# An added semaphore wait on GpSimd for VectorE's port instructions, in a fused attention, gated FFN and expert kernel

## The chip, the cores and the metric

The kernel runs on one core of a Trainium2 chip. The core has five engines with an instruction queue each: TensorE (PE, matrix products; PEld is its weight load), VectorE (DVE), ScalarE (ACT), GpSimd (POOL) and SyncE (SP, which issues the DMA transfers). Each queue runs in order, and the queues wait for one another by semaphores. The metric is the time of one execution on the device in microseconds, from runs on the chip.

## The reference

Three layers in float32 follow one another: causal attention with 12 heads, a gated feed-forward layer with a convolution over the sequence, and a sparse layer of four attention experts, of which each token takes the best two.

```python
B, H, S, D = 4, 12, 448, 64                      # batch, heads, sequence, head dimension
attn = softmax(mask(q @ k.T / 8)) @ v            # causal
x = attn as (B, S, 768)
h = relu(x @ w_in)                               # 768 -> 1024
conv = sum(conv_w[k] * shift(h, k - 1) for k in range(3))
x = (h * sigmoid(conv)) @ w_out                  # 1024 -> 768
logits = x @ w_gate                              # top 2 of 4 experts
for e in range(4):
    a = softmax(mask((x @ wq[e]) @ (x @ wk[e]).T / 8))
    out += gate[e] * (a @ (x @ wv[e]) @ wo[e])
```

## The kernel before

Every product in full precision is made of three products of rounded parts: a tensor is split into a high part (a rounded copy, helper `high`, L666 and the lines after it, shown as L670, L672 or L674 for ACT, DVE or POOL) and a low part (the remainder, helper `low`, L678). So beside every matmul there are copies and subtractions, and the kernel spreads them over ACT, DVE and POOL.

The work per batch is: six pairs of heads (`attention`), the feed-forward layer (`ffn_in`), the projections for the experts with w_out folded in (`project`), the experts (`experts`) and the output product (`output`). For one pair of heads, `scores` makes the scores on PE (L734), DVE masks them and takes the row maximum (L711, with the scores in PSUM as one input), ACT takes the exponentials and their sums (L715), DVE adds and inverts the sums (L753, L755), and the normalization is spread as eight to ten small multiplications over ACT (L760) and DVE or POOL (L763). `weigh` transposes the result on PE (L781), copies the transposes out of PSUM (ACT L670, DVE L672) and multiplies with the values (L814). L966 is the line of the three-part products.

In the first batch the weights are also unpacked from 64-bit words by three DVE instructions each (L885, L887, L889) and split into `slab` tiles; the parts are written to a scratch in HBM by SP (L907) and read back for later batches. In the feed-forward layer the convolution is done on DVE (L995) or ACT (L990), with the tanh on ACT (L1010) and the gate on DVE (L1003) or POOL (L1000, L1001).

The order of all this isn't that of the source. Every piece of work is noted as an operation (`P.op`) with the engines that could run it, a planned cost for each, what it reads and writes, and a `port`: a string with "V" in it for the DVE operations that the planner keeps apart from POOL's, and always with "G". The planner (`Plan.schedule`) then lays the operations in time, one list for each engine. An operation whose engine is in its `port` starts in the plan only when the last such operation, on either engine, has ended (L479, L518). So in the plan DVE's port operations and POOL's operations never overlap. On the chip nothing enforces that: the instructions are issued in the order of planned start times (L390, L391), and each engine then runs its own queue, waiting only for the data and buffers it needs.

DVE operations with "V" in their port are the copies, scalings and subtractions between SBUF tiles (those whose costs come from `copy_cost`, `scale_cost` and `two_cost`), the unpacking, the convolution and the gate. Operations with a PSUM input, such as L711 and the copies out of PSUM, have only "G".

Of the kernel before, what the change touches and what calls it, by code (L numbers as in the profile page):

```python
# [166 lines left out]
def noise(seed, n):  # L167

    x = (n * 2654435761 + seed * 40503 + 12345) & 0xFFFFFFFF
    for shift, factor in ((15, 0x2C1B3C6D), (12, 0x297A2D39), (15, 1)):  # L170
        x = ((x ^ x >> shift) * factor) & 0xFFFFFFFF
    return x / 2147483648.0 - 1.0
# [43 lines left out]
class Plan:  # L216
# [135 lines left out]
    def run(self):  # L352


        self.links()
        left = [(b, b.left) for t in self.tags.values() for b in t.made]
        kinds = {id(t.kind): (t.kind, dict(t.kind.free)) for t in self.tags.values()}

        def forward(rank):
            for b, n in left:  # L360
                b.left, b.ap = n, None
                for k in b.banks or ():
                    k.end, k.engine = 0.0, None
            for t in self.tags.values():
                t.next = t.live = 0
            for k, tiles in kinds.values():
                k.free = dict(tiles)
            return self.schedule(rank)

        rank = self.longest()  # L370
        length = forward(rank)
        best = (length, rank)
        for _ in range(ROUNDS):
            if length == float("inf"):
                break
            rank = self.backward()
            length = forward(rank)
            best = min(best, (length, rank))
        rank = list(best[1])
        forward(rank)  # L380
        begin = [o.start for o in self.ops]
        for seed, lo, hi, amp in SHIFTS:
            for o in self.ops:
                if seed < 0:
                    rank[o.n] += amp * (lo <= o.n < hi)
                elif lo <= begin[o.n] < hi:
                    rank[o.n] += amp * noise(seed, o.n)
        if SHIFTS and forward(rank) >= best[0]:
            forward(best[1])
        for o in sorted(self.ops, key=lambda o: (o.start, o.n)):  # L390
            o.fn(o.engine)  # L391

    def schedule(self, rank):
        for o in self.ops:
# [135 lines left out]
def on_scalar(n):  # L530
    return 0.05 + n / 1200


def on_vector(n):
    return 0.067 + n / 960
# [10 lines left out]
class Cost(dict):  # L546


    port = "V"
# [28 lines left out]
def attention_moe_moe(ctx: ExitStack, tc: tile.TileContext, qk, vv, w_in, cw, w_out, wqk, wvg, wo, out):  # L578
    nc = tc.nc
    ctx.enter_context(tc.manual_schedule())  # L580
    P = Plan()

    w1d = nc.dram_tensor("w1_scratch", (NF, 128, 2 * DM), F32, kind="Internal").ap()
    wod = nc.dram_tensor("wo_scratch", (2, 128, 2 * DM), F32, kind="Internal").ap()
# [65 lines left out]
    for name, kind, quota in (  # L650
# [9 lines left out]
            ("po", bank, PO), ("pf", sums, 2), ("fill", sums, 1)):  # L660
        P.tag(name, kind, quota)

# [20 lines left out]
    def scores(qk, j, e):  # L683
# [4 lines left out]
        whole = isinstance(qk, list)  # L688
        sbs = [{3: P.buf("sx"), 2: P.buf("sy")} for _ in range(2)]
        for sb in sbs:  # L690
            sb[0], sb[1] = sb[3], sb[2]
        st = P.buf("st")

        def bank(o, c):
            return sbs[o][c][:QN[c], COL[c]:COL[c] + Q0[c] + QN[c]]
# [5 lines left out]
        def kc(o, c):  # L701
            n = Q0[c] + QN[c]
            return slice(S - n, S) if o else slice(0, n)

        def weight(o, c):
# [11 lines left out]

            P.op({"V": on_vector(w)}, mx, r=[(sb[c], c)], w=[(e, (o, c)), (st, ("m", o, c))])
            P.op({"A": on_scalar(w) + 0.23}, ex, r=[(st, ("m", o, c))], w=[(e, (o, c)), (e, ("x", o, c)), (st, ("s", o, c))])

        if whole:
            for o, (qs, kh, r) in enumerate(qk):
                for c in ORDER:
                    w = Q0[c] + QN[c]
                    P.op({"T": 4 * w / 2400}, lambda _, o=o, c=c, w=w, qs=qs, kh=kh: nc.tensor.matmul(
                        bank(o, c), qs()[:, Q0[c]:Q0[c] + QN[c]], kh()[:, kc(o, c)], start=True, stop=True), r=r, w=[(sbs[o][c], c)])
# [490 lines left out]
```

## Time and profile before

| what | value |
|---|---|
| time, median of 3 runs | 534.32 us (533.75 to 536.55) |
| profiled execution, its own time | 535.11 us |
| its span, first to last instruction | 533.3 us |
| PE busy | 515.4 us (97%) |
| DVE busy | 421.6 us (79%), 1300 instructions |
| ACT busy | 357.7 us (67%) |
| POOL busy | 112.0 us (21%), 132 instructions |
| mean granted clock of TensorE | 0.992 |
| chain that ended last | PE 47%, DVE 25%, ACT 8%, issue 2% of the span |

The profiled execution is 0.8 us longer than the median of the runs. A busy time counts a moment once however many instructions overlap. PE's ends are modelled, so a busy PE isn't a PE at its peak; but its idle times are the time that another engine could give back. The chain that ended last runs through PE for long stretches and changes to DVE and ACT between them. A row of the timeline gives the start in us from the start of the span, the duration, the engine, the line, the operation, what it writes and reads with shapes, how many instructions are merged, and in brackets how long the engine was idle before it and which engine's instruction ended that.

### The profile page before, as it was taken

The page shows a single profiled execution, that of the slowest core. Times are in us where ns is not written, and L with a number is a line of the kernel's source. Part 1 is how long each engine was busy: PE and PEld are TensorE (multiplying, and loading weights), DVE is VectorE, ACT ScalarE, POOL GpSimd, SP SyncE. Part 2 cuts the span into 40 slices and gives each one's busy share as a digit, 9 for nine tenths or more (in the row PEclk, how much of TensorE's full clock was granted, in tenths as well). Part 3 has the DMA queues.
Part 4 walks back from the last instruction along what each step waited for, and adds up shares of the span by engine and source line. Part 5 has one row for each costly group of instructions (what it writes and reads, how often), then busy time and mean ns, then how long its engine had stood idle before and what let it go on. Part 6 is the DMA issues. An engine that isn't in the chain of part 4 may idle for free.

```text
span 533.3 us, 10436 instructions
## 1 busy us (share of the span) xinstructions
PE 515.4 (97%) x3554; PEld 436.2 (82%) x3556; DVE 421.6 (79%) x1300; ACT 357.7 (67%) x1058; POOL 112.0 (21%) x132
## 2 busy tenths in 40 slices
PE   8799999899899999899999999999999999999997
PEld 4678888778689898798898777998987778989875
DVE  6999599889798549999259999986389999842581
ACT  2876279789986557686249986755488867732572
POOL 3152017334232021160012511101114000000010
PEclk9999999899989999999999999999999999999999
DMA  9984246845587011374201573763003315610042
GB/s 239 256 222 135 63 149 195 255 120 206 167 246 201 23 36 37 139 250 163 68 2 46 146 219 84 249 215 87 1 1 113 117 49 194 221 59 1 10 154 104
DMA packets 63381, 69.92 MB, mean 131 GB/s; under 512 B 36576, under 2 KB 57312, under 8 KB 63328
## 3 DMA queue, kind: packets, MB, share of 16 engines
q1 hardware_dynamic: 63328, 69.26, 42.7%
q8 instruction: 28, 0.46, 0.4%
q14 instruction: 25, 0.20, 0.1%
HBM read 55.87 MB, written 13.37 MB: 130 GB/s over the span
## 4 chain that ended last, share of the span: by engine, by line
PE 47%; DVE 25%; ACT 8%; issue 2%; ACTq 0%; DVEq 0%
PE pf L966 34%; DVE e L711 7%; DVE e L763 5%; PE bank L814 5%; DVE z L672 4%; PE bank L781 3%; ACT e L715 3%; PE bank L734 3%; ACT e L760 2%; DVE pair L678 1%; DVE pair L672 1%; DVE work L995 1%; PE bank L966 1%; ACT z L670 1%; PE pf L1074 1%
## 5 line engine op out<-in xcount | busy, mean ns | idle before, releaser
L966 PE MATMUL pf<-pair,slab 128*128 128x448 f32 (+2 forms) x984 | 218.5, 368 | 4.3 <-ACT hp L984 2.7
L966 PEld LDWEIGHTS pf<-pair,slab 128*128 128x128 f32 x984 | 171.8, 189 | 22.2 <-ACT hp L984 3.7
L715 ACT ACTIVATE e<-e,stat 128x192 f32<-128x192 f32 (+3 forms) x256 | 127.1, 499 | 23.8 <-DVE stat L711 23.4
L711 DVE CUSTOM_DVE_ANT_0 e<-bank,mask 128x448 f32<-128x448 f32 (+3 forms) x256 | 92.1, 414 | 6.7 <-PE bank L734 6.5
L966 PE MATMUL pf<-pair,wqks 128*128 128x448 f32 x384 | 81.1, 369 | 0.0
L966 PEld LDWEIGHTS pf<-pair,wqks 128*128 128x128 f32 x384 | 71.4, 188 | 7.0 <-ACT pair L670 0.3
L781 PE MATMUL bank<-ident,e 128*128 128x128 f32 x448 | 70.7, 280 | 6.4 <-DVE stat L711 3.5
L678 POOL TENSOR_TENSOR pair<-work,pair 128x448 fp32r<-128x448 f32 (+1 forms) x39 | 48.6, 1260 | 105.6 <-PE bank L734 39.1
L781 PEld LDWEIGHTS bank<-ident,e 128*128 128x128 f32 x448 | 52.7, 142 | 16.9 <-DVE stat L711 3.6
L672 DVE COPY z<-bank 64x128 f32<-64x128 f32 (+2 forms) x121 | 48.7, 429 | 20.9 <-PE bank L781 16.7
L670 ACT ACTIVATE z<-bank 64x128 f32<-64x128 f32 (+2 forms) x135 | 45.8, 367 | 13.4 <-PE bank L814 7.4
L760 ACT ACTIVATE e<-e,stat 64x64 f32<-64x64 f32 (+3 forms) x116 | 49.4, 454 | 7.5 <-DVE stat L755 5.9
L734 PE MATMUL bank<-pair,pair 64*128 64x448 f32 (+3 forms) x576 | 49.6, 291 | 0.1
L814 PE MATMUL bank<-z,block 128*64 128x448 f32 (+3 forms) x384 | 48.7, 395 | 0.0
L715 ACT ACTIVATION_READ_ACCUMULATOR e<-e,stat 128x1 f32 (+1 forms) x256 | 48.5, 189 | 0.0
L995 DVE SCALAR_TENSOR_TENSOR work<-hp,cws,work 128x448 f32<-128x448 f32 x64 | 43.7, 694 | 3.9 <-ACT work L990 3.3
L734 PEld LDWEIGHTS bank<-pair,pair 64*128 64x128 f32 (+1 forms) x576 | 41.9, 172 | 3.3 <-issue 1.6
L814 PEld LDWEIGHTS bank<-z,block 128*64 128x64 f32 x384 | 27.3, 139 | 20.6 <-issue 11.5
L966 PE MATMUL pf<-wvs,pair 128*128 128x260 f32 x288 | 37.3, 286 | 0.0
L678 DVE TENSOR_TENSOR pair<-pf,pair 64x448 fp32r<-64x448 f32 (+1 forms) x24 | 15.0, 623 | 26.7 <-ACT pair L670 26.4
L966 PEld LDWEIGHTS pf<-wvs,pair 128*128 128x128 f32 x288 | 35.5, 188 | 0.3
L670 ACT ACTIVATE pair<-pf 64x448 fp32r<-64x448 f32 (+1 forms) x24 | 12.8, 541 | 32.3 <-PE pf L966 32.0
(99 smaller groups left out, 593.7 us busy)
## 6 DMA issues: line engine op xcount, KB each, us to landing
slab<-w_scratch SPq DMA_DIRECT2D x24, 768.0 KB, 4.6
work<-in_w_out SPq DMA_DIRECT2D x8, 768.0 KB, 4.8
work<-in_w_in SPq DMA_DIRECT2D x8, 768.0 KB, 5.7
w_scratch<-slab SPq DMA_DIRECT2D x8, 768.0 KB, 4.5
work<-in_qk SPq DMA_DIRECT2D x48, 112.0 KB, 3.4
work<-in_qk SPq DMA_DIRECT2D x24, 224.0 KB, 4.3
out<-work SPq DMA_DIRECT2D x24, 224.0 KB, 2.1
slab<-wo_scratch SPq DMA_DIRECT2D x6, 768.0 KB, 4.3
```

The source lines that it names most:

```text
L670: nc.scalar.activation(dst(), src(), AF.Copy)
L672: nc.vector.tensor_copy(dst(), src())
L678: return lambda e: engine(e).tensor_sub(dst(), src(), f32(h()))
L711: nc.vector.tensor_tensor_reduce(out=ec(o, c), in0=bank(o, c), in1=m, scale=-0.125, scalar=3.0e38, op0=OP.add, op1=OP.min, accum_out=st[ro ...
L715: nc.scalar.activation(ec(o, c), ec(o, c), AF.Exp, bias=st[rows, 0, o, c:c + 1], scale=-1.0, accum_out=st[rows, 1, o, c:c + 1])
L734: nc.tensor.matmul(bank(o, c), q(s)[own, Q0[c]:Q0[c] + QN[c]], k(t)[own, kc(o, c)], start=i == 0, stop=i == 2)
L760: nc.scalar.activation(dst(), src(), AF.Copy, scale=st[rows, 3, o, c:c + 1])
L763: engine(en).tensor_scalar(dst(), src(), st[rows, 3, o, c:c + 1], gate, op0=OP.mult, op1=OP.mult)
L781: P.op({"T": TURN}, lambda _: nc.tensor.transpose(dst(), src(), ident[:, :]), r=r, w=keys)
L814: nc.tensor.matmul(ps[own, S - n:S], v(k, o), z[:, 1024 * o + n0:1024 * o + n0 + n], start=k == 0, stop=k == 3)
L966: nc.tensor.matmul(out_ap(), a(), b(), start=first, stop=end), r=r, w=[(ps, 0)])
L995: return lambda _: nc.vector.scalar_tensor_tensor(cv[:, :S], hp[:, i:S + i], cws[:, fc, i:i + 1], cv[:, :S], op0=OP.mult, op1=OP.add)
```

## The change

When the program is written out in the planned order, the last DVE operation with "V" in its port is remembered. Each POOL operation whose planned start is less than 3 us behind the planned start of that DVE operation gets a dependency on the last instruction of it: the first POOL instruction of the operation waits by semaphore for that DVE instruction to be done. Nothing in the plan, in the order on any engine or in the work itself changes. DVE gets no wait for POOL.

```diff
+        body, near = self.nc.cur_bb.bb, None
         for o in sorted(self.ops, key=lambda o: (o.start, o.n)):
+            n = len(body.instructions)
             o.fn(o.engine)
+            new = body.instructions[n:]
+            if o.engine == "V" and "V" in o.port:
+                near = o, new[-1].name
+            elif o.engine == "G" and near and near[0].start > o.start - 3:
+                self.tc.add_manual_dep(new[0], near[1], mybir.DependencyInfo(mybir.DependencyClass.Sync, mybir.DependencyReason.DATA), reason="port")
@@
     P = Plan()
+    P.tc, P.nc = tc, nc
```

## Rows read from the trace of the kernel before

**Rows 1.** The page, part 1: busy us, share of the span, instructions of each engine

```profile
PE 515.4 (97%) x3554; PEld 436.2 (82%) x3556; DVE 421.6 (79%) x1300; ACT 357.7 (67%) x1058; POOL 112.0 (21%) x132
```

**Rows 2.** Windows: length, busy us (instructions) by engine, PEclk, DMA share, GB/s

```profile
100.00:150.00 50.00, 45.67 (x286) 37.55 (x287) 44.05 (x110) 43.46 (x122) 16.70 (x16) 0.93 0.60 187
```

**Rows 3.** Timeline of PE where it paused: start, us, [idle before, what ended it]

```profile
101.95 1.49 PE L781 MATMUL bank<-ident,e 128*128 128x128 f32 x6 [1.57 <-DVE pair L678]
...
131.03 1.29 PE L966 MATMUL pf<-pair,slab 128*128 128x448 f32 x5 [0.94 <-ACT hp L984]
...
144.87 0.47 PE L966 MATMUL pf<-pair,slab 128*128 128x448 f32 x1 [1.80 <-ACT hp L984]
...
217.16 1.14 PE L781 MATMUL bank<-ident,e 128*128 128x128 f32 x8 [1.38 <-DVE stat L711]
...
423.83 0.91 PE L781 MATMUL bank<-ident,e 128*128 128x128 f32 x6 [0.91 <-DVE stat L711]
```

**Rows 4.** Windows of PE alone: length, PE busy, PEclk, DMA share, GB/s

```profile
102.00:104.00 2.00, 2.00 (x9) 0.51 1.01 366
...
146.00:150.00 4.00, 3.99 (x18) 0.57 0.64 225
```

**Rows 5.** Timeline of POOL and DVE at 98 us; DVE's groups by form (busy, mean ns)

```profile
97.74 2.05 POOL L678 TENSOR_TENSOR slab<-work,slab 128x768 fp32r<-128x768 f32 x1 [0.29 <-ACT slab L670]
...
98.00 1.83 DVE L763 TENSOR_SCALAR e<-e,stat 64x64 f32<-64x64 f32 x1
...
L763 DVE TENSOR_SCALAR e<-e,stat 64x64 f32<-64x64 f32 x33 | 9.9, 306 | 1.0 <-ACT e L760 0.4
```

**Rows 6.** Timelines of POOL, DVE and ACT near 120 us; DVE's group of that form

```profile
119.92 1.84 POOL L678 TENSOR_TENSOR slab<-work,slab 128x768 fp32r<-128x768 f32 x1 [4.38 <-ACT slab L670]
122.25 1.86 POOL L678 TENSOR_TENSOR slab<-work,slab 128x768 fp32r<-128x768 f32 x1 [0.49 <-DVE slab L672]
...
120.12 2.05 DVE L672 CAST slab<-work 128x768 fp32r<-128x768 f32 x1
...
122.32 0.46 ACT L760 ACTIVATE e<-e,stat 128x192 f32<-128x192 f32 x1 [0.86 <-DVE stat L755]
...
L672 DVE CAST slab<-work 128x768 fp32r<-128x768 f32 x2 | 2.6, 1302 | 0.0
```

**Rows 7.** Timelines of POOL, DVE and PE near 214 us; two of DVE's groups

```profile
213.14 0.52 POOL L763 TENSOR_SCALAR e<-e,stat,coef 64x64 f32<-64x64 f32 x1
...
213.51 1.48 DVE L763 TENSOR_SCALAR e<-e,stat,coef 64x64 f32<-64x64 f32 x1
...
215.29 0.48 PE L781 MATMUL bank<-ident,e 128*128 128x128 f32 x2
...
L763 DVE TENSOR_SCALAR e<-e,stat,coef 64x64 f32<-64x64 f32 x28 | 9.5, 356 | 0.4
...
L711 DVE CUSTOM_DVE_ANT_0 e<-bank,mask 128x448 f32<-128x448 f32 x64 | 37.7, 615 | 4.6 <-PE bank L734 4.5
```

**Rows 8.** Timelines of POOL, DVE and PE near 420 us; DVE's group of that form

```profile
419.93 0.68 POOL L763 TENSOR_SCALAR e<-e,stat 128x384 f32<-128x384 f32 x1 [7.17 <-DVE stat L755]
...
420.07 0.65 DVE L763 TENSOR_SCALAR e<-e,stat 128x192 f32<-128x192 f32 x1
...
421.25 0.25 DVE L763 TENSOR_SCALAR e<-e,stat 64x64 f32<-64x64 f32 x1
...
421.53 0.38 PE L781 MATMUL bank<-ident,e 128*128 128x128 f32 x2
...
L763 DVE TENSOR_SCALAR e<-e,stat 128x192 f32<-128x192 f32 x16 | 6.0, 381 | 0.2
```

**Rows 9.** Timelines of POOL and DVE at 26 us

```profile
26.24 2.54 POOL L678 TENSOR_TENSOR pair<-work,pair 128x772 fp32r<-128x772 f32 x1 [6.99 <-ACT pair L670]
...
26.13 0.96 DVE L889 SCALAR_TENSOR_TENSOR work<-work 128x768 int32<-128x768 int32 x1
```

**Rows 10.** Timeline of POOL at 112 us

```profile
112.28 0.94 POOL L674 TENSOR_SCALAR pair<-work 128x896 fp32r<-128x896 f32 x1
```

## The prediction

> **What bounds the kernel now.** I read the busy times first. TensorE (PE) is busy for 515.4 of 533.3 us [rows 1], so a change on DVE and GpSimd (POOL) can give back little more than the time in which PE stands still. I then asked PE's timeline for the larger pauses, because each names who ended it [rows 3]: 1.57 us before 101.95 (ended by DVE), 0.94 and 1.80 us before 131.03 and 144.87 (ACT), 1.38 us before 217.16 and 0.91 us before 423.83 (DVE). Two of the five lie where three engines are full at once: between 100 and 150 us PE is busy for 45.67, DVE for 44.05 and ACT for 43.46 of 50 us [rows 2]. In that stretch the granted clock is 0.93, which is 50 x 0.07 = 3.5 us of full speed lost. It falls in two places, right behind the pause of 1.57 us (0.51 from 102 to 104) and right behind that of 1.80 us (0.57 from 146 to 150) [rows 4]: PE ran for a while at 1.2 instead of 2.4 GHz. The second drop costs 4 x 0.43 = 1.7 us, which leaves some 1.7 us for the first.
>
> Last I looked at what held DVE just before its pauses, and each time it was a POOL instruction running beside it. A norm of 64x64 takes 306 ns in the mean of 33; without the longest the mean is (33 x 0.306 - 1.83) / 32 = 0.26 us. That longest one took 1.83 us, from 98.00 to 99.83, while a POOL subtraction ran from 97.74 to 99.79 [rows 5]. A copy into slab took 2.05 us from 120.12, beside a POOL instruction that began 0.20 us earlier and ended at 121.76; the only other one of that form took 2 x 1.302 - 2.05 = 0.55 us [rows 6]. A norm with coef took 1.48 us where the other 27 took 0.31 [rows 7]. It goes the other way when DVE is first: POOL's subtraction at 26.24 began 0.11 us behind a DVE instruction that ended at 27.09, and took 2.54 us [rows 9]; its neighbour at 119.92, about as wide, took 1.84 [rows 6]. Whoever comes second stands still until the first is done.
>
> The Trainium skill (SBUF — State Buffer, Who interferes with whom) says the same: GpSimd and VectorE share a pair of ports as an exclusive lock for a whole instruction, and issue order decides who blocks. The rows agree. By that rule alone the wait changes who blocks, not how much; this is the first rival below.
>
> **What the change does.** It removes and reorders nothing. In the plan's order 121 POOL operations are issued and 70 of them stand less than 3 us of planned time behind a DVE instruction that can take the ports. Eleven of the 70 already wait, directly or through an earlier POOL instruction, for that DVE instruction or a later one. For the other 59 the wait is new. POOL is in order, so everything behind a waiting instruction waits too. The wait itself costs about 0.08 us: the POOL instruction at 122.25 already waits for the slab copy that ended at 122.17 [rows 6]. On POOL, which is busy 112 us of 533 [rows 1], that is covered unless PE waits for the result at once.
>
> **Place 1, 97.74 us.** POOL's subtraction now waits for the last of DVE's norms. DVE gets back 1.83 - 0.26 = 1.57 us, so the norms, the copy and the subtraction that PE waits for at 101.95 come that much sooner. PE paused for 1.57 us [rows 3]; I take 1.5. POOL's subtraction begins about 1.5 us later: the norm of 98.00 then ends near 98.3, two more norms follow, and the wait ends near 99.2. Its result is written out by SP's queue, and behind that write stand the next loads of q and k; POOL copies those at 112.28, and without an idle time before it [rows 10], so I take 1.5 us as covered there. If that cover were gone, POOL would read them up to 1.5 us late.
>
> **The clock behind it.** With the pause gone, nothing that I see in the rows is left to send PE to 1.2 GHz at 102. Bounds are 0 (it falls there all the same) and 1.7 us; I take 1.7, because both drops in this stretch come behind a long pause [rows 4]. The second drop stays in the sum: the pause of 1.80 us in front of it is ACT's.
>
> **Place 2, 119.92 us.** DVE's copy into slab is freed of 2.05 - 0.55 = 1.5 us. What waits for DVE next is ACT, which stood for 0.86 us before 122.32 [rows 6]; beyond that ACT is its own limit up to 144. Bounds 0 and 0.86; I take 0.8, near the upper end, since the row names DVE's reciprocal as what ended the wait and that sits right behind the copy. It comes out of PE's 0.94 us before 131.03. The two POOL subtractions move by some 0.8 and 0.3 us (1.84 each, from 120.7 instead of 119.92). PE's pauses behind them name ACT and not POOL [rows 3], so POOL was in time there; by how much no row here says, and the worst, that the gain of 0.8 is lost again, is the bound of 0.
>
> **Place 3, 213.5 us.** DVE's norm is freed of 1.48 - 0.31 = 1.17 us, directly in front of the scores that PE's pause of 1.38 us waits for through ACT. I take 1.15. POOL's three norms move by about as much. The first of them ends at 213.66 now and PE transposes it in a pair from 215.29 [rows 7], so it stays in time.
>
> **Place 4, 420 us.** A norm that took 0.65 us, (16 x 0.381 - 0.65) / 15 = 0.36 otherwise, is freed of 0.29 us in front of a pause of 0.91 [rows 3, 8]. I take 0.3.
>
> **What it costs.** In the first 40 us POOL splits weights that PE wants at once. At 26.24 POOL would begin at 27.09 + 0.08 and need 1.84 us instead of ending at 28.78, so it ends 0.2 us later, and so does the one behind it. Bounds 0 and 0.4; I take 0.2. Elsewhere POOL works ahead of the plan, and what it is held back by there I take as covered, since no larger pause of PE names POOL [rows 3]; what it costs without that cover is the second rival.
>
> The sum is 1.5 + 1.7 + 0.8 + 1.15 + 0.3 - 0.2 = 5.25, say 5.2 us. The profiled execution took 535.1 us, 0.8 more than the median of the runs shown (534.3). So the same execution would take 529.9, and the median 529.1.
>
> **Rivals.** *The lock is handed on.* POOL now begins just as the near DVE instruction ends, and then blocks the next DVE instruction instead; DVE loses again what it gained, and the time is 533.5 to 534.3. For it: both engines still want the same ports, and nothing makes DVE wait for POOL. Against it: behind the norms come the score reductions, and these keep their time whatever POOL does (64 of the widest average 615 ns [rows 7]). I give it 0.20.
>
> *POOL too late for PE* (the slower side). A head's norms are split over POOL and DVE, and PE transposes POOL's share in order. At 421.25 the last DVE norm begins and lasts 0.25 us. Held until 421.50 + 0.08, POOL's norm of 0.68 us ends at 422.26, but PE transposes it at 421.53 now [rows 8]: 0.7 us lost. This decides wherever DVE's norm does not itself come forward. Were four heads hit like this (my choice), with none of the gains, it would be 534.3 + 2.8 = 537. Against it: at place 3 there are 1.6 us to spare, and there and at place 4 DVE's norms do come forward. I give it 0.12.
>
> *The clock falls all the same.* The pauses go, but TensorE spends another stretch at 1.2 GHz somewhere else, 1.7 us: 530.8. I give it 0.10. *The wait does nothing*, because the DVE instruction had always ended: 534.3. The rows of the four places speak against it; 0.02.
>
> **How the numbers follow.** The forecast has the remaining 0.56. Its own range is 527.0 (the second clock drop goes as well, by a shift of its pause, 1.7 us, the cost in the first 40 us does not arise, 0.2, and place 3's pause of 1.38 goes whole, 0.2) to 531.6 (the first clock drop stays and place 2 gives nothing). A measurement of this kernel can tell about 0.5% from no change, 2.7 us. Faster by more than that, under 531.6: 0.56 + 0.10 = 0.66. Within: 0.20 + 0.02 = 0.22. Slower: 0.12. The range from 527.0 to 535.0 leaves out the slower rival and the tail of the forecast below it, together under 0.2.
>
> **What would show it.** In the profile after, DVE's norm near 98 us should take about 0.3 us and its copy into slab near 120 us about 0.55 us. PE should have no pause over 0.3 us near 100 us, and its clock there should be 1.00. The pause near 216 us should shrink below 0.4 us, and the one before 145 us should stay. The time that POOL waits for DVE should rise, without PE waiting for POOL. I am wrong if score reductions or slab subtractions now show the stretched durations, or if PE's pauses name POOL.

## The result, and the profile after

The kernel after takes 527.05 us (median of 4 runs, 526.54 to 527.90), the kernel before 534.15 (median of 4 runs, 533.75 to 536.55): a ratio of 0.9852, 95% interval 0.9825 to 0.9879. The gain of 7.1 us is in the direction of the forecast and 1.9 us larger than its 5.2; the time lies at the lower edge of the range. As a ratio to before it lies below it (527.0 of 534.32 is 0.9863). The profiled execution took 527.07 us, 8.0 less than that of before.

The helper lines in the kernel after are eight higher than before (L763 is now L771, L711 is L719, L678 is L686, L672 is L680, L781 is L789, L966 is L974). The first part of the page, to be held against [rows 1]:

```profile
PE 511.8 (97%) x3556; PEld 434.1 (83%) x3556; DVE 413.7 (79%) x1300; ACT 357.0 (68%) x1058; POOL 104.4 (20%) x132
```

DVE is busy for 7.9 us less and POOL for 7.6 us less, with the same work. What POOL spent as a stretched instruction it now spends idle, in front of the instruction. The second thing to see is PE: 3.6 us less busy time and, since the span fell by 8.0, 4.4 us less standing still. The two have different causes. The standing still is read from PE's timeline, the rows with a pause at the places of [rows 3] (start, us, in brackets the idle time before and what ended it):

```profile
126.80 3.92 PE L974 MATMUL pf<-pair,slab 128*128 128x448 f32 x18 [0.23 <-ACT hp L992]
...
140.63 0.47 PE L974 MATMUL pf<-pair,slab 128*128 128x448 f32 x1 [1.88 <-ACT hp L992]
...
210.46 1.14 PE L789 MATMUL bank<-ident,e 128*128 128x128 f32 x8 [0.59 <-DVE stat L719]
```

The pause of 1.57 us near 100 us and that of 0.91 near 423 have no row any more, 0.94 has become 0.23, 1.38 has become 0.59, and ACT's pause of 1.80 is still there (1.88). One more is gone that [rows 3] doesn't list; in the timeline of PE before it was:

```profile
304.07 1.09 PE L781 MATMUL bank<-ident,e 128*128 128x128 f32 x8 [0.56 <-DVE stat L711]
```

Together that is 1.57 + 0.71 + 0.79 + 0.56 + 0.91 = 4.5 us. Not all of it is gained. In the list of what PE waited for, which leaves out waits under 0.15 us, no line names POOL. But near 414 us PE's weight load (PEld) for the second pair of transposes, which had no wait in the trace of before, now waits for POOL's norm:

```profile
414.70 0.20 PEld L789 LDWEIGHTS bank<-ident,e 128*128 128x128 f32 x2 [0.40 <-POOL e L771]
```

From the first of these transposes to the six behind the old pause PE needed 2.79 us before (421.04 to 423.83) and needs 2.25 now (413.95 to 416.20). So of the pause of 0.91 us only 0.54 is gained.

The 3.6 us of PE's busy time are nearly all the clock. The window of [rows 2], with its columns, shows the full clock throughout, so also behind the pause of 1.88 us that stayed:

```profile
100.00:150.00 50.00, 47.83 (x330) 40.21 (x331) 43.58 (x113) 46.81 (x130) 18.11 (x17) 1.00 0.66 201
```

Lined up instruction by instruction, the lead of PE over the kernel before grows by 1.6 us behind the pause near 100 us, and by another 1.65 behind the pause near 143 us, which is as long as it was. These are the two stretches at 1.2 GHz of [rows 4]; the profiled execution of before had both of them and that of after neither.

On DVE and POOL, the rows that answer to [rows 5 to 8], with two rows of before behind them (97.48 and 419.77):

```profile
98.94 1.83 POOL L686 TENSOR_TENSOR slab<-work,slab 128x768 fp32r<-128x768 f32 x1 [1.56 <-ACT z L678]
...
97.08 1.72 DVE L771 TENSOR_SCALAR e<-e,stat 128x192 f32<-128x192 f32 x6
...
116.60 0.56 DVE L680 CAST slab<-work 128x768 fp32r<-128x768 f32 x1
...
206.41 1.09 POOL L771 TENSOR_SCALAR e<-e,stat,coef 128x320 f32<-128x320 f32 x2 [18.78 <-DVE e L771]
208.83 1.67 POOL L771 TENSOR_SCALAR e<-e,stat,coef 64x64 f32<-64x64 f32 x3 [1.32 <-DVE e L771]
...
207.05 1.58 DVE L771 TENSOR_SCALAR e<-e,stat,coef 64x64 f32<-64x64 f32 x4 [0.26 <-POOL e L771]
...
412.69 1.18 DVE L771 TENSOR_SCALAR e<-e,stat 128x320 f32<-128x320 f32 x4
...
97.48 3.22 DVE L763 TENSOR_SCALAR e<-e,stat 128x192 f32<-128x192 f32 x6
419.77 1.72 DVE L763 TENSOR_SCALAR e<-e,stat 128x320 f32<-128x320 f32 x4
```

Near 97 us six norms of DVE (merged in one row, which shows the shape of the first) take 1.72 us; the same six took 3.22 in the trace of before. POOL's subtraction starts behind them, at 98.94, and takes 1.83 us. The copy into slab takes 0.56 us where it took 2.05. Four norms near 413 us take 1.18 us where they took 1.72. By form, the small norms of DVE fell from 306 and 356 ns [rows 5, 7] to 247 and 317, and the score reduction did not move (615 ns [rows 7], now 617):

```profile
L771 DVE TENSOR_SCALAR e<-e,stat 64x64 f32<-64x64 f32 x33 | 8.0, 247 | 0.6
L771 DVE TENSOR_SCALAR e<-e,stat,coef 64x64 f32<-64x64 f32 x28 | 8.4, 317 | 0.6 <-POOL e L771 0.3
...
L719 DVE CUSTOM_DVE_ANT_0 e<-bank,mask 128x448 f32<-128x448 f32 x64 | 37.7, 617 | 5.7 <-PE bank L742 5.6
```

### The profile page after: what moved, and what is told of

Its sections match the earlier page's. It is cut to its first block, busy times and chain, and to the rows that moved or that the text cites. A ratio compares the mean times of both kernels' runs of the same rounds, so it can differ in the third digit from the quotient of the medians.

```text
span 525.3 us, 10440 instructions
## 1 busy us (share of the span) xinstructions
PE 511.8 (97%) x3556; PEld 434.1 (83%) x3556; DVE 413.7 (79%) x1300; ACT 357.0 (68%) x1058; POOL 104.4 (20%) x132
## 4 chain that ended last, share of the span: by engine, by line
PE 49%; DVE 22%; ACT 7%; issue 2%; DMA 1%; POOL 1%; POOLq 0%; ACTq 0%; DVEq 0%
PE pf L974 38%; DVE e L719 6%; DVE z L680 4%; PE bank L822 4%; DVE e L771 4%; PE bank L789 3%; PE bank L742 3%; ACT e L768 2%; ACT e L723 2%; DVE pair L686 1%; PE bank L974 1%; ACT z L678 1%; DMA work<-in_qk 1%; DVE pair L680 1%; PE pf L1082 1%
## 5 line engine op out<-in xcount | busy, mean ns | idle before, releaser
L974 PE MATMUL pf<-pair,slab 128*128 128x448 f32 (+2 forms) x984 | 218.2, 368 | 3.5 <-ACT hp L992 2.1
L974 PEld LDWEIGHTS pf<-pair,slab 128*128 128x128 f32 x984 | 171.2, 188 | 21.7 <-ACT hp L992 2.6
L719 DVE CUSTOM_DVE_ANT_0 e<-bank,mask 128x448 f32<-128x448 f32 (+3 forms) x256 | 92.2, 415 | 7.6 <-PE bank L742 7.4
L974 PE MATMUL pf<-pair,wqks 128*128 128x448 f32 x384 | 80.7, 368 | 0.0
L974 PEld LDWEIGHTS pf<-pair,wqks 128*128 128x128 f32 x384 | 71.6, 188 | 6.3
L789 PE MATMUL bank<-ident,e 128*128 128x128 f32 x448 | 69.5, 277 | 2.5 <-DVE stat L719 1.2
L686 POOL TENSOR_TENSOR pair<-work,pair 128x448 fp32r<-128x448 f32 (+1 forms) x39 | 47.2, 1223 | 101.9 <-PE bank L742 39.4
L680 DVE COPY z<-bank 64x128 f32<-64x128 f32 (+2 forms) x121 | 48.6, 428 | 19.6 <-PE bank L789 15.4
L789 PEld LDWEIGHTS bank<-ident,e 128*128 128x128 f32 x448 | 52.2, 140 | 12.5 <-DVE stat L719 1.6
L678 ACT ACTIVATE z<-bank 64x128 f32<-64x128 f32 (+2 forms) x135 | 45.7, 367 | 10.4 <-PE bank L822 6.8
L822 PE MATMUL bank<-z,block 128*64 128x448 f32 (+3 forms) x384 | 47.1, 386 | 0.0
L974 PE MATMUL pf<-wvs,pair 128*128 128x260 f32 x288 | 37.3, 286 | 0.0
L686 DVE TENSOR_TENSOR pair<-pf,pair 64x448 fp32r<-64x448 f32 (+1 forms) x24 | 15.0, 623 | 26.7 <-ACT pair L678 26.4
L974 PEld LDWEIGHTS pf<-wvs,pair 128*128 128x128 f32 x288 | 35.5, 188 | 0.3
L678 ACT ACTIVATE pair<-pf 64x448 fp32r<-64x448 f32 (+1 forms) x24 | 12.8, 540 | 32.4 <-PE pf L974 32.1
```

Source lines behind the costliest of these rows:

```text
L678: nc.scalar.activation(dst(), src(), AF.Copy)
L680: nc.vector.tensor_copy(dst(), src())
L686: return lambda e: engine(e).tensor_sub(dst(), src(), f32(h()))
L719: nc.vector.tensor_tensor_reduce(out=ec(o, c), in0=bank(o, c), in1=m, scale=-0.125, scalar=3.0e38, op0=OP.add, op1=OP.min, accum_out=st[ro ...
L789: P.op({"T": TURN}, lambda _: nc.tensor.transpose(dst(), src(), ident[:, :]), r=r, w=keys)
L822: nc.tensor.matmul(ps[own, S - n:S], v(k, o), z[:, 1024 * o + n0:1024 * o + n0 + n], start=k == 0, stop=k == 3)
```

## The experiments

The theory: DVE's instructions in front of PE's pauses lose time because POOL begins an instruction just before them; the wait gives that time back at a few places, and the pauses shrink. The rivals: POOL, being held, takes the ports from a later DVE instruction, so the gain is handed on; all of DVE's freed time counts, and not only that in front of PE's pauses; and, for the part of the gain that is clock, that it is not tied to the pauses that went but to what the executions happened to show.

Five of the kernels are made from the kernel after by a condition on the number of the planned operation (`o.n`), e4_half from the kernel before, and e6_both and e7_wide by other edits of the kernel after: 947 is POOL's subtraction at 97.74 [rows 5], 981 the one at 119.92 [rows 6], 1768, 1769 and 1776 are POOL's norms near 213 us [rows 7], 2522 and 2524 two near 301 us, 3573 and 3574 two at 420 us [rows 8]. Since the mean granted clock differs from execution to execution, the table has beside the medians the difference at full clock: from each time, span x (1 - mean clock) is taken off, and the mean is compared with that of the kernel before on the same chip. 95% intervals are given. The executions of one row ran on one chip; a difference between two rows can be one between chips.

| kernel | runs | median us | ratio to before, interval | mean clock | clock of before there | us to before at full clock |
|---|---|---|---|---|---|---|
| e1_place1 | 12 | 531.89 | 0.9976 (0.9956 to 0.9996) | 0.9972 | 0.9976 | -1.4 +- 0.7 |
| e2_rest | 6 | 529.91 | 0.9926 (0.9898 to 0.9954) | 0.9968 | 0.9976 | -4.3 +- 0.9 |
| e3_places | 6 | 527.91 | 0.9903 (0.9871 to 0.9934) | 0.9985 | 0.9976 | -4.6 +- 0.9 |
| e4_half | 10 | 532.48 | 0.9981 (0.9960 to 1.0002) | 0.9978 | 0.9976 | -1.1 +- 0.8 |
| e5_places34 | 12 | 530.29 | 0.9962 (0.9936 to 0.9987) | 0.9981 | 0.9980 | -2.4 +- 0.7 |
| e6_both | 6 | 528.78 | 0.9921 (0.9897 to 0.9945) | 0.9998 | 0.9980 | -3.6 +- 0.6 |
| e7_wide | 7 | 529.53 | 0.9930 (0.9903 to 0.9958) | 0.9986 | 0.9980 | -3.5 +- 0.8 |
| e8_place2 | 12 | 534.36 | 1.0005 (0.9976 to 1.0034) | 0.9966 | 0.9980 | -0.3 +- 0.6 |
| a1_after | 6 | 526.74 | 0.9867 (0.9838 to 0.9897) | 0.9995 | 0.9965 | -5.8 +- 0.8 |

**e1_place1: the wait on the subtraction of place 1 alone.**

```diff
-            elif o.engine == "G" and near and near[0].start > o.start - 3:
+            elif o.engine == "G" and near and near[0].start > o.start - 3 and o.n == 947:
```

> The kernel before with one of the 59 new waits only: the POOL subtraction into slab at 97.74 us waits for DVE's norms. Few places decide (mine): the pause of PE of 1.57 us at 100 us goes, and with it the stretch at 1.2 GHz behind it (1.6 us), so about 3.1 us less in an execution that had that stretch, 1.5 in one that had not; DVE's norm near 98 us takes under 0.4 us. Rival, all of DVE's freed time counts (about 8 us over 59 waits): one wait gives under 1 us. Rival, a pause of PE does not set the clock: 1.5 us in the pause, and the stretch at 1.2 GHz stays behind the shifted place.

Measured: 531.89 us, 1.4 us less than before at full clock. The trace has the six norms in 1.63 us, no pause near 100 us, and the pauses further on at their old size. The timelines of DVE and PE, and a window of PE behind the pause of 1.88 us:

```profile
98.09 1.63 DVE L771 TENSOR_SCALAR e<-e,stat 128x192 f32<-128x192 f32 x6
...
142.31 0.47 PE L974 MATMUL pf<-pair,slab 128*128 128x448 f32 x1 [1.88 <-ACT hp L992]
...
140.00:146.00 6.00, 4.10 (x30) 1.00 0.72 253
```

So place 1 gives what its pause was, 1.5 us within the interval. Its clock term doesn't come with it: over 12 executions the mean clock is 0.9972, against 0.9976 for the kernel before beside it. And in this trace the clock stays whole behind a pause of 1.88 us, where it fell behind one of 1.80 in [rows 4].

**e2_rest: all waits but this one.**

```diff
-            elif o.engine == "G" and near and near[0].start > o.start - 3:
+            elif o.engine == "G" and near and near[0].start > o.start - 3 and o.n != 947:
```

> The changed kernel without the wait of the POOL subtraction at 97.74 us; the 58 other waits stay. Few places decide: about 3.1 us slower than the changed kernel, the pause at 100 us and the stretch at 1.2 GHz behind it are back; 4 to 5 us less than the kernel before. Rival, all of DVE's freed time counts: within 1 us of the changed kernel.

Measured: 529.91 us. Place 1 is back as it was: POOL at 97.44, the six norms in 3.31 us, and PE's pause with a stretch at half clock behind it. The pause of 1.88 us in front of 143.97 has none. DVE, PE and a window of PE:

```profile
97.18 3.31 DVE L771 TENSOR_SCALAR e<-e,stat 128x192 f32<-128x192 f32 x6
...
101.74 1.20 PE L789 MATMUL bank<-ident,e 128*128 128x128 f32 x6 [1.66 <-DVE pair L686]
...
102.00:106.00 4.00, 4.00 (x18) 0.57 1.04 279
```

At full clock e1 and e2 add up to 1.4 + 4.3 = 5.7 us, as much as the whole change (5.8): within about 1.2 us there is no sign that place 1 and the rest depend on one another.

**e3_places: nine waits, at the four places of the prediction and at 301 us.**

```diff
-            elif o.engine == "G" and near and near[0].start > o.start - 3:
+            elif o.engine == "G" and near and near[0].start > o.start - 3 and o.n in (947, 981, 1776, 1768, 1769, 2522, 2524, 3573, 3574):
```

> The kernel before with nine of the new waits: the POOL operations at 97.74, 119.92, 213.14 to 214.29, 300.96 and 301.73, 419.93 and 420.59 us. Few places decide: 6 to 7.5 us less, nearly the whole gain of the change. Rival, all of DVE's freed time counts: nine of 59 waits give 2 us or less.

Measured: 527.91 us, 4.6 us less at full clock and 5.05 in the means, short of the 6 to 7.5 that were expected. Nine waits bring most of the gain of all of them (5.8); the difference of 1.2 has an interval as wide as itself, so these times don't settle whether the others do anything. The traces do: see the table below, in the part on why. This trace also has a stretch at half clock in a place where none was before, behind a pause of PE near 28 us (POOL, DVE, PE, and a window of PE):

```profile
24.77 2.38 POOL L686 TENSOR_TENSOR pair<-work,pair 128x772 fp32r<-128x772 f32 x1 [6.16 <-ACT pair L678]
...
25.49 2.47 DVE L897 SCALAR_TENSOR_TENSOR work<-work 128x768 int32<-128x768 int32 x1
...
28.02 0.44 PE L789 MATMUL bank<-ident,work 128*128 128x128 f32 x2 [1.82 <-DVE work L897]
...
29.00:31.00 2.00, 2.00 (x12) 0.53 0.76 225
```

The pause is the one of place 1 over again. POOL's subtraction of [rows 9], which e3 doesn't hold, came ahead of DVE's last unpacking instruction here, and that took 2.47 us where it took 0.96 in the trace of before. The same stands in the traces of e5 and e8 (2.48 us, and PE's pause of 1.82); in those of before, e1 and e4 POOL came second. In the five traces of kernels with this wait (after, a1, e2, e6, e7) DVE's instruction takes 0.96.

**e4_half: the kernel before, without any wait, with POOL's subtraction of place 1 cut to half its width.** It leaves out columns 384 to 767 of that one part of the split weights.

```diff
+            self.half = o.n == 947
...
-        return lambda e: engine(e).tensor_sub(dst(), src(), f32(h()))
+        def fn(e):
+            n = DM // 2 if P.half else None
+            engine(e).tensor_sub(dst()[:, :n], src()[:, :n], f32(h())[:, :n])
+        return fn
```

> The kernel before, no new wait; the POOL subtraction into slab at 97.74 us handles 384 of its 768 columns, the others are left out. The port is held for the length of POOL's instruction (mine): it takes about 1.0 instead of 2.05 us, DVE's norm beside it about 0.75 instead of 1.83, ending within 0.1 us of POOL's end, and PE's pause at 100 us shrinks by about 1.1 to 0.5 us. Rival, the norm waits for its own data: it still takes 1.8 us and the pause stays at 1.5.

Measured: 532.48 us, 1.1 us less at full clock. POOL's instruction is 1.21 us long, and DVE's six norms take 2.39 us: between the 3.22 beside the whole one and the 1.72 without. The norm that stood beside it began at 97.35 and ended at 98.35, 0.05 us behind POOL's end at 98.30, so its length follows POOL's. PE's pause is halved as well. Timelines of POOL, DVE (the six norms merged, then that norm alone) and PE:

```profile
97.09 1.21 POOL L681 TENSOR_TENSOR slab<-work,slab 128x384 fp32r<-128x384 f32 x1 [0.30 <-ACT slab L671]
...
96.83 2.39 DVE L767 TENSOR_SCALAR e<-e,stat 128x192 f32<-128x192 f32 x6
97.35 1.00 DVE L767 TENSOR_SCALAR e<-e,stat 64x64 f32<-64x64 f32 x1
...
100.47 0.88 PE L785 MATMUL bank<-ident,e 128*128 128x128 f32 x6 [0.74 <-DVE pair L681]
```

This measures the disputed cost by itself, without any wait: the norm isn't slowed by a share, it stands until POOL is done. Alone it takes some 0.26 us, so it stood for 0.74, and PE's pause is 0.74 us.

**e5_places34: the seven waits near 213, 301 and 420 us.**

```diff
-            elif o.engine == "G" and near and near[0].start > o.start - 3:
+            elif o.engine == "G" and near and near[0].start > o.start - 3 and o.n in (1776, 1768, 1769, 2522, 2524, 3573, 3574):
```

> The kernel before with the new wait at seven POOL norms only: 213.14 to 214.29, 300.96 and 301.73, 419.93 and 420.59 us (places 3 and 4 and the one at 301, which the prediction left out). Few places decide: the pauses of PE there shrink as in the changed kernel, by 0.8 us at 216, by about 0.7 at 304 and by about 0.8 at 423, together some 2.2 us at an equal clock. The prediction's own terms would make it 1.15 + 0 + 0.3 = 1.45. Rival, POOL's delayed norms come too late for PE there: the pauses then name POOL, and the time is that of the kernel before or longer.

Measured: 530.29 us, 2.4 us less at full clock. The pauses of places 1 and 2 and that of 1.80 us are as before, the later ones are small or gone, and the four norms of place 3, 2.64 us in the trace of before (the first row), take 1.47 here (the others):

```profile
212.69 2.64 DVE L763 TENSOR_SCALAR e<-e,stat,coef 64x64 f32<-64x64 f32 x4
...
211.54 1.47 DVE L771 TENSOR_SCALAR e<-e,stat,coef 64x64 f32<-64x64 f32 x4
...
104.05 0.88 PE L789 MATMUL bank<-ident,e 128*128 128x128 f32 x6 [1.57 <-DVE pair L686]
145.34 0.47 PE L974 MATMUL pf<-pair,slab 128*128 128x448 f32 x1 [1.80 <-ACT hp L992]
214.84 1.14 PE L789 MATMUL bank<-ident,e 128*128 128x128 f32 x8 [0.26 <-DVE stat L719]
300.91 0.44 PE L789 MATMUL bank<-ident,e 128*128 128x128 f32 x2 [0.30 <-POOL e L771]
```

Two things follow. Here 1.38 us of pause became 0.26, better than the 0.59 of the whole change, which also holds POOL's first two norms at that place: there POOL starts them 0.66 us behind the start of DVE's 128x320 norm (206.41 against 205.75; in this kernel 0.18), and DVE then stands for 0.26 us in front of its four norms and needs 1.58 for them. That is the rival of the lock handed on, at the size of 0.3 us. And at 300.91 PE waits for POOL, 0.30 us: the slower rival, at one place. The mean clock of these 12 executions is 0.9981, that of before 0.9980, and in this trace both old pauses of 1.57 and 1.80 us, and the one of 1.82 near 28 us, stand without a stretch at half clock.

**e8_place2: the wait at 119.92 us alone.**

```diff
-            elif o.engine == "G" and near and near[0].start > o.start - 3:
+            elif o.engine == "G" and near and near[0].start > o.start - 3 and o.n == 981:
```

> The kernel before with the new wait at the POOL subtraction at 119.92 us only. Few places decide: DVE's copy into slab takes about 0.56 instead of 2.05 us, PE's pause of 0.94 us before 131.03 falls to about 0.2, the one of 1.80 before 144.87 stays: 0.7 us less at an equal clock. If ACT is its own limit throughout, nothing. If a pause of PE of 1.6 us or more always lowers the clock behind it, the stretches at 102 and 146 us are at 1.2 GHz in this profile as in the one of before; if it only can, one or both are missing.

Measured: 534.36 us, at full clock 0.3 +- 0.6 us less. The copy takes 0.56 us and PE's pause fell from 0.94 to 0.23, as in the kernel after, but 0.7 us lies at the edge of what these runs can tell. The stretch at half clock behind 1.57 us is there, that behind 1.79 us is not, and a third stands behind the pause of 1.82 us near 28 us. DVE's copy, PE's timeline, a window behind its first pause and one behind its last:

```profile
122.31 0.56 DVE L680 CAST slab<-work 128x768 fp32r<-128x768 f32 x1
...
104.14 0.88 PE L789 MATMUL bank<-ident,e 128*128 128x128 f32 x6 [1.57 <-DVE pair L686]
132.50 3.98 PE L974 MATMUL pf<-pair,slab 128*128 128x448 f32 x18 [0.23 <-ACT hp L992]
146.33 0.47 PE L974 MATMUL pf<-pair,slab 128*128 128x448 f32 x1 [1.79 <-ACT hp L992]
...
104.00:108.00 4.00, 3.86 (x17) 0.61 1.05 300
144.00:150.00 6.00, 4.19 (x31) 1.00 0.70 249
```

**e6_both: DVE also waits for POOL's last instruction, where the plan has it less than 3 us ahead.**

```diff
             if o.engine == "V" and "V" in o.port:
                 near = o, new[-1].name
+                if pool and pool[0].start > o.start - 3:
+                    self.tc.add_manual_dep(new[0], pool[1], mybir.DependencyInfo(mybir.DependencyClass.Sync, mybir.DependencyReason.DATA), reason="port")
...
+            if o.engine == "G":
+                pool = o, new[-1].name
```

> The changed kernel, and DVE's port instructions wait in the same way for the last POOL instruction that the plan puts under 3 us ahead: planned order enforced from both sides. The lock only makes the second one wait (mine): where POOL is first DVE stands still anyway, so nothing is gained; each place where POOL is late for its own reasons now holds DVE too: 0 to 3 us slower than the changed kernel. Rival, overlap itself costs (both engines lose when they meet): a further gain of 1 us or more over the changed kernel.

Measured: 528.78 us, 3.6 us less than before at full clock: the wait in this direction gives 2.2 us of the 5.8 back (5.8 - 3.6, measured on two chips, with an interval of about 1). DVE is busy for 409.7 us, less than in the kernel after, but it now stands in front of its instructions instead. Its list of waits has (total, times, longest)

```profile
DVE e L775 <- POOL e L775: 2.1, 5, 0.7
```

and that of PE has 1.0 us for POOL, 0.8 of it at once.

**e7_wide: a limit of 12 us of planned time instead of 3.**

```diff
-            elif o.engine == "G" and near and near[0].start > o.start - 3:
+            elif o.engine == "G" and near and near[0].start > o.start - 12:
```

> The changed kernel with 12 instead of 3 us as the limit, so that POOL operations that the plan puts up to 12 us behind a port instruction of DVE wait for it too. Few places decide: these DVE instructions have mostly ended by then, so the same as the changed kernel within 0.5 us at an equal clock. Rival, each wait gives a share: a further gain.

Measured: 529.53 us, 3.5 us less at full clock, 2.3 us worse than the kernel after (on another chip, with an interval of about 1.2), where the same within 0.5 was expected. In the kernel after, POOL's copy of q and k starts at 184.35. Here it is held until a DVE instruction ends, begins at 190.14, and lands beside the expert gate's small instructions on SBUF tiles. POOL, then DVE, then PE:

```profile
190.14 0.94 POOL L682 TENSOR_SCALAR pair<-work 128x896 fp32r<-128x896 f32 x1 [21.69 <-DVE values L680]
191.17 1.14 POOL L686 TENSOR_TENSOR pair<-work,pair 128x448 fp32r<-128x448 f32 x1
...
190.30 0.86 DVE L1113 TENSOR_TENSOR work<-work 128x64 f32<-128x64 f32 x1
191.19 1.20 DVE L1114 TENSOR_TENSOR work<-work,tri 128x64 f32<-128x64 f32 x1
192.42 1.06 DVE L1115 TENSOR_TENSOR work<-work 128x64 f32<-128x64 f32 x1
...
196.06 0.33 PE L789 MATMUL bank<-ident,e 128*128 128x128 f32 x1 [0.84 <-DVE stat L719]
196.80 0.88 PE L789 MATMUL bank<-ident,e 128*128 128x128 f32 x6 [0.42 <-DVE stat L719]
```

Three instructions that take 0.23 us each in the kernel after take 3.1 together, and PE, which has no pause there in the kernel after, pauses for 1.26 us. Here the lock is handed on. The Trainium skill (SBUF — State Buffer, Who interferes with whom) says that the order of issue decides who blocks, not the shape of the operation. The rows agree: an instruction of 0.23 us stood for 1.20, because POOL's was there 0.02 us earlier (191.17 and 191.19).

**a1_after: the kernel after once more, beside the kernel before on one chip.** Without an edit.

> The changed kernel once more, without an edit, beside the kernel before on one chip. So far it was timed in four executions, all with a mean clock near 1.0, while the kernel before lost 0.0024 of its clock in the mean (about 1.3 us of its time), and four executions can have been lucky. Theory (the freed DVE instructions give about 5.4 us at an equal clock, the clock adds what the executions happen to show, 0 to 1.7 us): median 527 to 528, ratio to the kernel before 0.986 to 0.990, and, with the lost clock taken off both, 4.9 to 5.9 us less. Rival (a part of the gain was the luck of four executions, and the nine waits of the experiment with places 1 to 4 were already everything): 528.5 to 529.5, 3.8 to 4.6 us less with the lost clock taken off. Rival (the time of the kernel after is a matter of the chip it ran on): a ratio outside 0.9825 to 0.9879 by more than 0.004.

Measured: 526.74 us against 533.68, ratio 0.9867 (0.9838 to 0.9897); 5.8 +- 0.8 us less at full clock. The rest of the difference of the means (534.08 - 526.68 = 7.4 us), 1.6 us, is clock: 0.9995 against 0.9965. The gain was no luck of four executions. At full clock it is larger than the theory's 5.4, by less than its interval.

## Why the prediction was right or wrong

**The mechanism, right.** DVE stood behind POOL at the places named, for as long as the part of POOL's instruction that was left (e4), and the wait removes that. Norms, copy and score reductions came out as the prediction's last part had them. One of its signs failed: PE's pause near 216 us was to fall below 0.4 us and is 0.59.

**The step that failed: the places were taken from PE's five larger pauses alone.** What DVE loses to POOL elsewhere was put at nothing, without a reason. PE has the same 3556 weight loads in the same order in every trace. The table gives by how much PE gains on the trace of before in each stretch, from the start times of the same loads, with the stretches at half clock taken off in both (us, rounded; the first column in the time of before).

| stretch | prediction | after | a1_after | e3_places | e1_place1 |
|---|---|---|---|---|---|
| 0 to 24 | | 0.2 | 0.2 | 0.6 | -0.7 |
| 24 to 40, the cost | -0.2 | -0.3 | -0.3 | -0.8 | 0.0 |
| 40 to 98 | | 0.5 | 0.5 | 0.0 | 0.1 |
| 98 to 109, place 1 | 1.5 | 1.4 | 1.3 | 1.5 | 1.5 |
| 109 to 140, place 2 | 0.8 | 0.8 | 0.8 | 0.8 | 0.1 |
| 140 to 210 | | -0.2 | -0.1 | -0.1 | -0.1 |
| 210 to 222, place 3 | 1.15 | 0.8 | 0.8 | 1.2 | 0.1 |
| 222 to 298 | | 0.3 | 0.6 | 0.0 | 0.0 |
| 298 to 310, four norms at 301 | | 0.6 | 0.6 | 0.4 | 0.0 |
| 310 to 420 | | -0.5 | 0.0 | 0.0 | -0.6 |
| 420 to 425, place 4 | 0.3 | 0.5 | 0.5 | 0.5 | 0.0 |
| 425 to 442 | | 0.4 | 0.4 | 0.0 | 0.0 |
| 442 to the end | | 0.0 | 0.3 | 0.4 | 0.3 |
| sum without the clock | 3.55 | 4.6 | 5.7 | 4.6 | 0.6 |

The stretches 0 to 24, 310 to 420 and 442 to the end differ as much between kernels that have no wait there, so these differences are not the waits'. The others repeat. At 301 us the wait gives some 0.6 us, and in three stretches where PE's timeline shows hardly a pause (one, of 0.29 us) the waits give 0.5, 0.3 to 0.6 and 0.4, in the traces of after, a1, e2 and e7 and in none of e1, e3, e4, e5 and e8. That is about 2 us for which the sum has nothing. The cause looks the same: in each of the three a DVE instruction that lay beside POOL is shorter with the waits. Near 234 us, for instance (POOL and DVE of before, DVE of after), a copy stood beside POOL:

```profile
234.06 1.55 POOL L678 TENSOR_TENSOR pair<-work,pair 128x448 fp32r<-128x448 f32 x1
...
234.50 1.35 DVE L672 CAST pair<-work 128x448 fp32r<-128x448 f32 x1
...
228.18 0.39 DVE L680 CAST pair<-work 128x448 fp32r<-128x448 f32 x1 [0.88 <-POOL work L1009]
```

So the sum without the clock, 3.55, was short of the 5.8 +- 0.8 that the runs gave, and its clock term was too large. The total came nearer to the measured gain by that second error, which is luck.

**The clock behind place 1, wrong.** The step read 1.7 us off one execution in which both long pauses of [rows 4] had a stretch at half clock behind them, and tied the loss to the pause. The runs show that a stretch at half clock comes behind some pauses of that length and not behind others: behind 1.57 and 1.80 in before, 1.66 in e2, 1.82 in e3, 1.57 and 1.82 in e8; not behind 1.57, 1.80 and 1.82 in e5, 1.88 in e1, e2 and after, 1.79 in e8, 2.04 in after. A pause is so a chance of 1.7 us, not a price. Over all its 58 executions in the experiments, before ran at a mean clock of 0.9976, which is 0.0024 x 532 = 1.3 us lost; the kernel after, over 10 executions, at 0.9994, 0.3 us lost. The whole change is therefore worth some 1.0 us in clock, and e1, which removes the very pause to which the prediction gave it, shows none. The profiled pair shows some 3.4, because before had two such stretches in that execution and after none. That is also most of why the profiled execution gained more than the sum.

**Place 1, right.** 1.5 us were put down; the pause of 1.57 went whole, and the wait alone gave 1.4 +- 0.7 (e1).

**Place 2, the pause right, the time not shown.** 0.8 us were put down, the pause shrank by 0.71 in the kernel after and in e8, but e8 measured 0.3 +- 0.6.

**Place 3, mis-sized.** 1.15 us were put down, 0.79 came. With the last three norms alone held, 1.12 came (e5). The prediction looked for the norm that is freed and not for the two that POOL runs before it, which are held as well and then stand in DVE's way.

**Place 4, mis-sized.** The step took one norm (0.29 us). The row of before that it rests on shows one of four; all four together fell from 1.72 to 1.18, which is 0.54, and that is what PE gained. At 301 us the same pattern, four norms from 1.58 to 1.18 and a pause of 0.56, stood in the trace and not in the sum. The waits at places 3, 4 and 301 together gave 2.4 +- 0.7 (e5), against 1.45 in the sum.

**The cost in the first 40 us, right in size and with an unseen other side.** Between 24 and 40 us PE loses 0.3 in the traces of after and a1, and 0.2 was put down. But this holds against executions in which POOL comes second at 26 us. Where it comes first and no wait holds it, as in the traces of e3, e5 and e8, PE loses 0.8 to 1.0 us there, and in two of the three another 1.7 by the clock; the wait prevents that.

**The count of new waits, too high.** The 70 operations stand behind only 36 different DVE instructions: several POOL operations wait for the same one, and in an in-order queue the first of them does it for all.

**The rivals.** The lock is handed on at place 3 (0.3 us) and, where POOL is held for longer, at 190 us in e7 (some 1.9 us). POOL too late for PE shows at 300.91 in e5 (0.30 us), in e6, in a1 twice in the first 40 us (0.21 and 0.22, where before has one of 0.42), and at place 4 in the kernel after, where the second pair of transposes comes 0.27 us later behind the first than before. Neither decides the time of the change as made. That all of DVE's freed time counts, few places or many, doesn't fit e3: nine waits gave 4.6 us, where that rival had 2 or less.

**What stays open.** How often POOL comes first at 26 us isn't known: it did in three of the six traces without that wait, and no kernel has that wait alone. So its share of the gain isn't shown, nor whether it explains why e1's executions lost as much clock as before's. The smaller waits near 45, 234 and 430 us weren't run alone either. One trace was taken of each kernel, and two of the kernel after. A version that holds only the last three norms of place 3 should give 0.3 us more than the change, too little for these runs to tell, and wasn't tried.

## What to carry to other kernels

When two engines exclude one another for an instruction's length, look in front of each pause of the bound engine for a small instruction stretched beside a long one of the other engine; the stretch that reaches the pause, summed over all its neighbours in the same row, is about what a wait can give back. Do this where the bound engine shows a small pause or none too: here such places held some 2 of the 5.8 us. Put the wait on the engine that has time, and look at what the other does next: held too long (e7), or in both directions (e6), some 40% of the gain was lost again. Before a term of a sum is taken from the clock, look at several executions: the profiled execution of before had lost three times what its runs lose in the mean. And look at several traces for who comes first: at 26 us that changed from trace to trace.

## What was not expected of the hardware

TensorE's granted clock fell to 0.5 behind pauses as short as 1.57 us in some executions, and stayed at 1.00 behind pauses of 2.04 (after) and 2.32 us (e1) in others of almost the same program; each such stretch cost some 1.7 us. The order of POOL and DVE at 26 us differed between traces of kernels that do the same there, and with it the length of one DVE instruction, 0.96 or 2.48 us. And a wait cost little by itself: POOL's instruction that waited for DVE's end at 26.86 began at 27.00 in the kernel after. These are the two rows, POOL and DVE, that answer to [rows 9]:

```profile
27.00 4.76 POOL L686 TENSOR_TENSOR pair<-work,pair 128x772 fp32r<-128x772 f32 x3 [7.01 <-DVE work L897]
...
25.90 0.96 DVE L897 SCALAR_TENSOR_TENSOR work<-work 128x768 int32<-128x768 int32 x1
```

Three POOL instructions take 4.76 us there instead of the 5.46 that the row of three in the trace of before has, because the first no longer stands behind DVE: it ends at 31.76 for 31.70, so the queue lost 0.06 us by a wait of 0.76.
